# Output tiles of a gated MLP placed between the products of the next group, with PSUM banks of long and short use

## The chip, the cores and the metric

The kernel runs on one core of a Trainium2 chip. Its time is what the device takes for one execution, in microseconds (us). Five engines work side by side, each in its own program order: TensorE (PE, with its weight loads as PEld), VectorE (DVE), ScalarE (ACT), GpSimd (POOL) and SyncE (SP, which issues the transfers). An instruction starts when all before it on its engine have started and the semaphores that it names have been raised.

## What is computed

Clustered attention on 2 x 8 heads of 768 rows (1536 tokens of 512 values), then two MLPs without a bias; the change is in the second:

```python
def _moe_ref(x, w1, w2, w3, w_out):
    a = x @ w1
    b = x @ w2
    h = a * b @ w3
    return (h @ w_out).astype(np.float32)

def _moe2_ref(x, w_gate, w_val, w_out):        # 512 -> 1536 -> 512
    gate = 1.0 / (1.0 + np.exp(-(x @ w_gate)))
    val = x @ w_val
    return (gate * val @ w_out).astype(np.float32)
```

The weights of the MLPs come as 64-bit floats.

## The kernel before

Every matmul is done in three: each operand is split into a high part that the matmul takes exactly and a low part, and mm3 (L64 to L67) adds high x high, high x low and low x high into one PSUM bank. The high part is a copy or cast (by ACT or POOL), the low part a subtraction (by DVE or POOL).

**The second MLP** works on the 1536 hidden columns in six groups M of 256. For a group, `quads(M, 0)` makes the gates and `quads(M, 1)` the values. Each is a scheme of seven products (a to g) of half-size blocks in place of eight, once for each half p of the tokens: 14 products a0, a1, b0, b1, c0, c1, d0, e0, d1, e1, g0, f0, g1, f1, each 6 matmuls of 384 columns. Products a, c, e and g of one half add into one bank (names p4_..._a0, a1), b and f into another (b0, b1), d has its own (d0, d1). Partial sums are read between the steps: a **snapshot** s (ACT, L910) copies the a bank before the next product adds to it; DVE adds snapshots to later banks (L918, or L923) and, for the values, multiplies by the gate (L924, called a gate below). Of each finished block u = gate x value ACT then casts the high half (L929) and DVE subtracts the low half (L933). Twelve **output tiles** `out_unit(M, t)` of 128 tokens, 6 matmuls of 512 columns each, multiply u by the group's rows of w_out; DVE adds each to acc (L992; the first group's are copied by ACT, L990).

**The order around the change** is written out. The program of PE is a list of items (a product, or half a long one, or an output tile); `then(f, later)` puts f behind the item `later` places on, and `when(time, f)` puts f where the item at that time stands, on a clock of ticks, one tick being 12 matmuls of 512 columns. So the tables of times set the order on each engine, and the semaphores the rest. Before, the output tiles 0 to 5 of a group stand right behind its values, and 6 to 11 behind the gates of the next group:

```python
    for M in range(MG // GS):
        for w in range(2):
            ask_out(GS * M + w, at - 0.5)
            quads(M, w)
            if M or w:
                for t in range(6):
                    out_unit(M - 1 + w, t + 6 * (1 - w))
```

**Conversions.** A 64-bit weight tile is fetched by SP as raw words (512 KB), ACT takes two pieces of it (L836, L838), DVE clips, shifts and merges (L839, L842, L843, by way of a PSUM tile t), and POOL adds (L844). `ask_forms` then makes the seven weight forms: sums by POOL (L872), high halves by ACT (L886), low halves by POOL (L892). `ask_out` does the same for w_out.

**PSUM** has eight banks: six for products in one rotation (pool ps), two for t. A bank is used again when its last reader is done. **Before the second MLP**, the first one's last stage (`y_unit`) reads the split of g (`split_g`: high half by POOL or ACT, low half ghl by DVE, L59).

Of the kernel before, what the change touches and what calls it, by code (L numbers as in the profile page):

```python
# [27 lines left out]
def tile_cluster_attention__then__moe__then__gated_moe(  # L28
# [625 lines left out]

    def then(f, later=1):
        items[-1][1].append((later, f))
# [171 lines left out]
    def value_steps(src, name, key):  # L828
# [11 lines left out]
        yield  # L840
        t = cvp["pool"].tile([128, n], U32, tag="t", name=f"{name}_t", bufs=2)
        nc.vector.tensor_scalar(out=t, in0=a, scalar1=3, scalar2=0x3FFFFFF8, op0=ALU.logical_shift_left, op1=ALU.bitwise_and)  # L842
# [4 lines left out]
    def convert_at(time, src, name, key):  # L847
        steps = value_steps(src, name, key)
        for after in (-2.3, 0, 0.4, 1.0):
            when(time + after, lambda: next(steps, None))  # L850

    def ask_forms(M, w, start):
        key = (M, w)
        lead = 2.2 if M or w else 8.0
        for i in range(2):
            convert_at(start - lead - 2.8 + 1.2 * i, w_gv[2 * M + i, w], f"wgv{2 * M + i}_{w}", (key, i))
        half = [slice(0, 256), slice(256, 512)]
# [36 lines left out]

        for f, (pos, _, _) in A.items():
            time = start + pos * 6 * UNIT / TICK - lead
            if f in "bcef":
# [3 lines left out]

    def quads(M, w):
        key = (M, w)
# [9 lines left out]
        def combined(p, unit, mt, src, n):  # L913
# [12 lines left out]
            def hi():  # L926
                if (M, p, unit) not in us:
                    us[M, p, unit] = late["snap"].tile([128, GS, 2, UNIT], F32R, tag="u", name=f"u{M}_{p}_{unit}", bufs=4)
                nc.scalar.copy(us[M, p, unit][:, mt, 0], g)  # L929

            def lo():
                u = us[M, p, unit][:, mt]
                nc.vector.tensor_tensor(out=u[:, 1], in0=g, in1=u[:, 0], op=ALU.subtract)  # L933
# [6 lines left out]
            else:  # L940
                then(total)
                then(hi, 2)
                then(lo, 3)

        for step in "a0 a1 b0 b1 c0 c1 d0 e0 d1 e1 g0 f0 g1 f1".split():
            f, p = step[0], int(step[1])
            here = {"d": Y, "b": Z, "f": Z}.get(f, X)
            if f in "abd":
                here[p] = bank(f"p4_{M}_{w}_{f}{p}")[:, 0:UNIT]
            form = A[f][2]  # L950
            product(here[p], [lambda k=k, f=f: (a_hl[key, f][:, 0, 128 * k : 128 * k + 128], a_hl[key, f][:, 1, 128 * k : 128 * k + 128]) for k in range(2)],
                    [lambda k=k, p=p, form=form: y_form(p, form, k) for k in range(2)], f in "abd")
            if f == "a":
                then(snapshot(1, p))
            elif f == "c":
                then(snapshot(2, p))
# [10 lines left out]
    def ask_out(m, start):  # L967
        convert_at(start, w_out2[m], f"wo2_{m}", ("o", m))
# [5 lines left out]
        def lo():  # L974
            nc.gpsimd.tensor_tensor(out=wo2[m][:, 1], in0=outs["o", m], in1=wo2[m][:, 0], op=ALU.subtract)
        when(start + 2.0, hi)
        when(start + 2.3, lo)

    def out_unit(M, t):
        p, r = divmod(t, 6)  # L980
        unit, r = divmod(r, 3)
        tt = slice(128 * r, 128 * r + 128)
        bk = bank(f"p5_{M}_{t}")
        product(bk, [lambda i=i: (us[M, p, unit][:, i, 0, tt], us[M, p, unit][:, i, 1, tt]) for i in range(GS)],
                [lambda i=i: (wo2[GS * M + i][:, 0], wo2[GS * M + i][:, 1]) for i in range(GS)])
# [38 lines left out]
    for n, (work, posts, start, end) in enumerate(items):  # L1024
# [8 lines left out]
        work()  # L1033
        for f in due.pop(n, ()):
            f()
        while events and events[0][0] < end:
            events.pop(0)[2]()
        for later, f in posts:
            due.setdefault(n + later, []).append(f)
    for k in sorted(due):  # L1040
        for f in due[k]:
            f()
# [60 lines left out]
```

## Time and profile before

| | |
|---|---|
| median of 3 runs | 806.33 us (805.41 to 807.14) |
| the profiled execution, its own time | 806.35 us |
| its span, first to last instruction | 804.6 us |
| PE busy | 764.2 us (95%) |
| DVE, ACT, POOL busy | 558.5, 470.1, 399.6 us |
| mean granted clock of PE | 0.987 |

The views name an instruction by its line of the kernel, its engine and "output <- inputs" by tile names; a number in square brackets is the idle time of the engine before it and what ended it. A matmul's end is modelled, so that one is drawn longer than the distance to the next.

### The profile page before, as it was taken

How to read it: one execution, taken by the hardware profiler on the slowest of the kernel's cores; microseconds unless marked ns; L12 is line 12 of the kernel's file. 1: busy time of each engine (PE TensorE's matmuls, PEld its weight loads, DVE VectorE, ACT ScalarE, POOL GpSimd, SP SyncE). 2: the span in 40 equal slices, each digit the busy share in tenths (PEclk: the TensorE clock that was granted, in tenths of full speed). 3: DMA queues.
4: the chain of work that ended last, by engine and by line, in shares of the span. 5: the costliest groups of instructions: out<-in, count | busy, mean ns of one | idle time of the engine just before them, and what ended most of it. 6: DMA issues, size and time to landing. Idle time of an engine off the chain costs nothing.

```text
span 804.6 us, 12228 instructions
## 1 busy us (share of the span) xinstructions
PE 764.2 (95%) x4293; PEld 687.3 (85%) x4293; DVE 558.5 (69%) x895; ACT 470.1 (58%) x980; POOL 399.6 (50%) x418
## 2 busy tenths in 40 slices
PE   7999999998999999999999999989999899998997
PEld 7888888888998888888889988979889798897996
DVE  6798989898976665677642666574565856658555
ACT  3788788879885645455531354756654455454540
POOL 3447777777663456333320344835466354552540
PEclk9899999999999999999999999999999999999999
DMA  8766767666513333344320010312122120221004
GB/s 221 195 179 168 190 193 172 167 173 153 129 50 114 129 131 132 105 139 136 122 76 0 1 53 1 105 52 70 36 79 79 52 79 28 79 79 53 27 0 158
DMA packets 28893, 82.63 MB, mean 103 GB/s; under 512 B 4800, under 2 KB 4960, under 8 KB 28832
## 3 DMA queue, kind: packets, MB, share of 16 engines
q1 hardware_dynamic: 28832, 81.86, 34.4%
q8 instruction: 34, 0.56, 0.3%
q14 instruction: 27, 0.22, 0.1%
HBM read 52.49 MB, written 3.19 MB: 69 GB/s over the span
## 4 chain that ended last, share of the span: by engine, by line
PE 69%; DVE 14%; ACT 5%; issue 4%; DMA 3%; POOL 3%; SPq 1%; ACTq 0%; DVEq 0%; POOLq 0%
PE p L67 12%; PE p L66 11%; PE p L65 11%; PE pt L343 3%; PE p_a L65 3%; PE p_a L67 3%; PE p_a L66 3%; PE av L384 3%; DVE gate L924 2%; PE av L385 2%; DVE s L923 2%; PE w34p L65 2%; PE w34p L66 2%; PE w34p L67 2%; DMA xb<-xa 2%
## 5 line engine op out<-in xcount | busy, mean ns | idle before, releaser
L322 DVE TENSOR_REDUCE nm<-s 128x1 f32<-128x768 f32 x96 | 90.3, 942 | 11.4 <-PE s L315 10.9
L333 ACT ACTIVATE e<-s,nm 128x768 f32<-128x768 f32 x96 | 87.3, 909 | 14.6 <-DVE nm L322 13.9
L384 PE MATMUL av<-ph,vx 128*128 128x256 f32 x288 | 80.6, 309 | 11.1 <-ACT xa L393 10.5
L372 DVE TENSOR_TENSOR pl<-pt,ph 128x512 fp32r<-128x512 f32 x120 | 80.0, 682 | 11.6 <-ACT ph L361 10.3
L844 POOL TENSOR_TENSOR wgv_a<-wgv_f 128x512 uint32<-128x512 uint32 x24 | 26.6, 1108 | 120.2 <-ACT wgv_f L838 51.8
L361 ACT CAST ph<-pt 128x512 fp32r<-128x512 f32 x120 | 69.2, 593 | 23.5 <-PE pt L343 23.0
L343 PE MATMUL pt<-ident,e 128*128 128x128 f32 x576 | 80.2, 275 | 0.7 <-DVE pl L372 0.7
L67 PE MATMUL p<-x,w 128*128 128x512 f32 x192 | 74.7, 389 | 0.0
L66 PE MATMUL p<-x,w 128*128 128x512 f32 x192 | 74.7, 389 | 0.0
L65 PE MATMUL p<-x,w 128*128 128x512 f32 x192 | 74.7, 389 | 0.0
L343 PEld LDWEIGHTS pt<-ident,e 128*128 128x128 f32 x576 | 67.7, 143 | 5.8 <-PE pt L343 0.9
L385 PE MATMUL av<-pl,vx 128*128 128x256 f32 x288 | 72.6, 281 | 0.0
L67 PE MATMUL p<-wo,u 128*128 128x512 f32 x144 | 59.6, 414 | 13.1 <-DVE u L933 13.1
L384 PEld LDWEIGHTS av<-ph,vx 128*128 128x128 f32 x288 | 54.3, 188 | 18.9 <-ACT xa L393 8.8
L106 POOL TENSOR_TENSOR w_a<-w_f 128x512 uint32<-128x512 uint32 x32 | 34.7, 1085 | 62.6 <-DVE w_f L105 28.8
L66 PE MATMUL p<-wo,u 128*128 128x512 f32 x144 | 58.7, 407 | 0.0
L65 PE MATMUL p<-wo,u 128*128 128x512 f32 x144 | 58.7, 407 | 0.0
L385 PEld LDWEIGHTS av<-pl,vx 128*128 128x128 f32 x288 | 54.6, 190 | 0.1
L992 DVE TENSOR_TENSOR acc<-p,acc 128x512 f32<-128x512 f32 x60 | 40.6, 686 | 17.1 <-PE p L67 17.1
L929 ACT CAST u<-gate 128x384 fp32r<-128x384 f32 x48 | 24.6, 512 | 47.0 <-DVE gate L924 47.0
L910 ACT COPY s<-p_a 128x384 f32<-128x384 f32 x72 | 34.1, 475 | 27.9 <-PE p_a L67 27.8
L67 PEld LDWEIGHTS p<-wo,u 128*128 128x128 f32 x144 | 28.4, 197 | 21.8 <-DVE u L933 15.7
(229 smaller groups left out, 2315.5 us busy)
## 6 DMA issues: line engine op xcount, KB each, us to landing
wgv_f<-in_w_gv_dram SPq DMA_DIRECT2D x24, 512.0 KB, 3.2
wo_f<-in_w_out_dram SPq DMA_DIRECT2D x20, 512.0 KB, 3.2
w_f<-in_w_dram SPq DMA_DIRECT2D x16, 512.0 KB, 4.8
w_f<-in_w3T_dram SPq DMA_DIRECT2D x16, 512.0 KB, 4.2
raw<-in_qkT_dram SPq DMA_DIRECT2D x16, 384.0 KB, 3.2
vraw<-in_v_dram SPq DMA_DIRECT2D x8, 384.0 KB
QH<-hi SPq DMA_DIRECT2D x16, 192.0 KB, 4.7
KH<-hi SPq DMA_DIRECT2D x16, 192.0 KB, 3.6
```

What stands on the lines that cost most here:

```text
L65: nc.tensor.matmul(ps, whi, xhi, start=start, stop=False, skip_group_check=more)
L66: nc.tensor.matmul(ps, whi, xlo, start=False, stop=False, skip_group_check=more)
L67: nc.tensor.matmul(ps, wlo, xhi, start=False, stop=stop, skip_group_check=more)
L106: nc.gpsimd.tensor_tensor(out=a, in0=high, in1=low, op=ALU.add)
L322: nc.vector.tensor_reduce(out=nms[j], in_=sps[j][:, 0:S], axis=AX.X, op=ALU.max, negate=True)
L333: nc.scalar.activation(et, sps.pop(j)[:, 0:S], AF.Exp, bias=nms.pop(j), accum_out=acc_x[pr, "sum"][:, at : at + 1])
L343: nc.tensor.transpose(pt[:, kk, 128 * t : 128 * t + 128], exps[2 * i + t][:, k0 : k0 + 128], ident)
L361: nc.scalar.copy(ph, pt)
L372: nc.vector.tensor_tensor(out=pl, in0=src, in1=ph, op=ALU.subtract)
L384: nc.tensor.matmul(avs[i], w, ph[:, kk, :], start=kt == 0, stop=False)
L385: nc.tensor.matmul(avs[i], w, pl[:, kk, :], start=False, stop=kt == KT - 1)
L992: nc.vector.tensor_tensor(out=acc[:, t, :], in0=bk, in1=acc[:, t, :], op=ALU.add)
```

## The change

Output tiles no longer stand in rows of six. Group M's tiles 0 to 5 stand behind the sixth to eleventh product of the gates of group M+1, tiles 6 to 11 behind the products 1, 3, 4, 5, 6 and 7 (from 0) of its values; the last group keeps three of them for after its values, ahead of its own twelve. PSUM is divided anew: four long banks (a0, a1, b0, b1, each always the same one), three short ones (d and the output tiles), one for t. In the earlier stages the seven rotate. Posts behind an item get a second key (`turn`), by which snapshots come first; the cast of u's high half moves one item later, its low half one more. Conversions and forms get new times, w_out's are asked for within the values. split_g has 12 places for its halves in place of 10 (two of them in x's old memory), and splits four before the last unit in place of two.

```diff
-            t = cvp["pool"].tile([128, n], U32, tag="t", name=f"{name}_t", bufs=2)
+            t = cvp["pool"].tile([128, n], U32, tag="t", name=f"{name}_t", bufs=1)
...
-    def bank(name):
-        return ps.tile([128, 512], F32, tag="p", name=name)
+    LONG, SHORT = 4, 3
+    banks = 0
+
+    def bank(name, tag=None):
+        nonlocal banks
+        if not tag:
+            tag = "long" if banks % (LONG + SHORT) < LONG else "short"
+            banks += 1
+        return ps.tile([128, 512], F32, tag=tag, name=name, bufs=LONG if tag == "long" else SHORT)
...
-        hl = late["e"].tile([128, 2, UNIT], F32R, tag="e", name=f"ghl{v}_{m}", bufs=10)
+        n = (MF * v + m) % 12
+        if n < 10:
+            hl = late["e"].tile([128, 2, UNIT], F32R, tag="e", name=f"ghl{v}_{m}", bufs=10)
+        else:
+            hl = x_flat[:, PAIR * (n + 4) : PAIR * (n + 5)].rearrange("p (h c) -> p h c", h=2)
...
-                    when(at - 2 * half + 0.3 * k if k < 2 else at + half * (1 + (k > 5)), lambda k=k, v=v: split_g(v + 1, k))
+                    when(at - 2 * half + 0.4 * k if k < 4 else at + half, lambda k=k, v=v: split_g(v + 1, k))
...
-        lead = 2.2 if M or w else 8.0
+        if M == w == 0:
+            asked = (-10.8, -9.6)
+            ready = {f: A[f][0] * 6 * UNIT / TICK - 8.0 for f in A}
+        elif w == 0:
+            asked = (-6.2, -5.0)
+            ready = dict(a=-2.2, b=-1.6, c=-0.6, d=0.0, e=0.6, g=1.2, f=1.8)
+        else:
+            asked = (-5.0, -3.8) if M else (-4.6, -3.4)
+            ready = dict(a=-2.2, b=-1.8, c=-1.4, d=-1.0, e=-0.2, g=0.2, f=0.6)
...
-                then(hi, 2)
-                then(lo, 3)
+                then(hi, 3)
+                then(lo, 4, 2)
...
-                here[p] = bank(f"p4_{M}_{w}_{f}{p}")[:, 0:UNIT]
+                here[p] = bank(f"p4_{M}_{w}_{f}{p}", "short" if f == "d" else "long")[:, 0:UNIT]
...
-                then(snapshot(3, p))
+                then(snapshot(3, p), 1, 0)
...
+            for M_, t in (between or {}).get(n, ()):
+                out_unit(M_, t, "short")
...
+    LAST_M = MG // GS - 1
     for M in range(MG // GS):
-        for w in range(2):
-            ask_out(GS * M + w, at - 0.5)
-            quads(M, w)
-            if M or w:
-                for t in range(6):
-                    out_unit(M - 1 + w, t + 6 * (1 - w))
-    for t in range(6, 12):
-        out_unit(MG // GS - 1, t)
+        first = {5 + i: [(M - 1, i)] for i in range(6)} if M else {}
...
+        quads(M, 0, first)
...
+        then_tiles = {n: [(M - 1, 6 + i)] for i, n in enumerate((1, 3, 4, 5, 6, 7))} if M else {}
+        if M == LAST_M:
+            then_tiles = {n: [(M - 1, 6 + i)] for i, n in enumerate((1, 3, 4))}
+        quads(M, 1, then_tiles)
+    banks = 0
+    for t in range(9, 12):
+        out_unit(LAST_M - 1, t, "short")
+    for t in range(12):
+        out_unit(LAST_M, t)
```

**PE, end of the values of group 3.** Before, the last matmuls of product f1 (p4_3_1_b1) and then the group's first output tile (p5_3_0), which reads u:

```order
L65 MATMUL p4_3_1_b1_4095<-yb22_1_6081,a3_1_3_7628 128x384
L66 MATMUL p4_3_1_b1_4095<-yb22_1_6081,a3_1_3_7628 128x384
L67 MATMUL p4_3_1_b1_4095<-yb22_1_6081,a3_1_3_7628 128x384
L65 MATMUL p5_3_0_4098<-wo2_6_7404,u3_0_0_7655 128x512
L66 MATMUL p5_3_0_4098<-wo2_6_7404,u3_0_0_7655 128x512
L67 MATMUL p5_3_0_4098<-wo2_6_7404,u3_0_0_7655 128x512
```

In the changed kernel, the same place, where the first gate product of group 4 (p4_4_0_a0) follows:

```order
L65 MATMUL p4_3_1_b1_4090<-yb22_1_6085,a3_1_3_7536 128x384
L66 MATMUL p4_3_1_b1_4090<-yb22_1_6085,a3_1_3_7536 128x384
L67 MATMUL p4_3_1_b1_4090<-yb22_1_6085,a3_1_3_7536 128x384
L65 MATMUL p4_4_0_a0_4098<-x_153,a4_0_0_7676 128x384
L66 MATMUL p4_4_0_a0_4098<-x_153,a4_0_0_7676 128x384
```

The output tiles that stood there have moved six products on, and a0 needs a bank of the products just finished.

**DVE, the same tail.** Before, from the gate of g0 (it reads p4_3_1_a0) to the first low half of u that the output tile waits for (u3_0_0 from gate0_1); wgv8 and wgv9 are conversions:

```order
L924 TENSOR_TENSOR gate0_1_4016<-p4_3_1_a0_4092,gate0_1_4016 128x384
L842 TENSOR_SCALAR wgv8_0_t_7699<-wgv8_0_a_7661 128x512
L843 SCALAR_TENSOR_TENSOR wgv8_0_f64_7599<-wgv8_0_f64_7599,wgv8_0_t_7699 128x512
L933 TENSOR_TENSOR u3_1_1_7696<-gate1_1_4018,u3_1_1_7696 128x384
L923 TENSOR_TENSOR s3_1_2_0_7626<-p4_3_1_b0_4094,s3_1_2_0_7626 128x384
L924 TENSOR_TENSOR gate0_0_4015<-s3_1_2_0_7626,gate0_0_4015 128x384
L839 TENSOR_SCALAR wgv9_0_a_7703<-wgv9_0_a_7703 128x512
L933 TENSOR_TENSOR u3_0_0_7655<-gate0_1_4016,u3_0_0_7655 128x384
```

In the changed kernel, from the sum of d0 (L944 is the old L923, L945 the old L924, L952 the old L933, L1024 the old L992) to the gate of g1, which empties p4_3_1_a1:

```order
L1024 TENSOR_TENSOR acc_6078<-p5_2_11_4096,acc_6078 128x512
L952 TENSOR_TENSOR u3_0_0_7662<-gate0_0_4015,u3_0_0_7662 128x384
L944 TENSOR_TENSOR s3_1_1_1_7544<-p4_3_1_d1_4097,s3_1_1_1_7544 128x384
L945 TENSOR_TENSOR gate1_0_4017<-s3_1_1_1_7544,gate1_0_4017 128x384
L944 TENSOR_TENSOR s3_1_3_1_7696<-p4_3_1_b1_4090,s3_1_3_1_7696 128x384
L945 TENSOR_TENSOR gate1_1_4018<-s3_1_3_1_7696,gate1_1_4018 128x384
L952 TENSOR_TENSOR u3_0_1_7685<-gate0_1_4016,u3_0_1_7685 128x384
L945 TENSOR_TENSOR gate0_1_4016<-p4_3_1_a0_4086,gate0_1_4016 128x384
L944 TENSOR_TENSOR s3_1_2_0_7600<-p4_3_1_b0_4089,s3_1_2_0_7600 128x384
L945 TENSOR_TENSOR gate0_0_4015<-s3_1_2_0_7600,gate0_0_4015 128x384
L952 TENSOR_TENSOR u3_1_0_7710<-gate1_0_4017,u3_1_0_7710 128x384
L945 TENSOR_TENSOR gate1_1_4018<-p4_3_1_a1_4087,gate1_1_4018 128x384
```

No conversion stands between them any more, and one add of an output tile does.

**ACT, around the last snapshot of the values** (s3_1_3_1, of product e1). Before:

```order
L910 COPY s3_1_3_0_7657<-p4_3_1_a0_4092 128x384
L836 ACTIVATE wgv8_0_a_7661<-wgv8_0_f64_7599 128x512
L929 CAST u3_0_1_7670<-gate0_1_4016 128x384
L838 ACTIVATE wgv8_0_f64_7599<-wgv8_0_f64_7599 128x512
L929 CAST u3_1_0_7683<-gate1_0_4017 128x384
L910 COPY s3_1_3_1_7685<-p4_3_1_a1_4093 128x384
```

In the changed kernel (L931 is the old L910, L948 the old L929, L907 the old L886):

```order
L931 COPY s3_1_3_0_7660<-p4_3_1_a0_4086 128x384
L948 CAST u3_0_0_7662<-gate0_0_4015 128x384
L907 CAST a4_0_0_7676<-wgv8_0_a_7582 128x256
L948 CAST u3_0_1_7685<-gate0_1_4016 128x384
L907 CAST a4_0_0_7676<-sum4_0_b_7666 128x256
L931 COPY s3_1_3_1_7696<-p4_3_1_a1_4087 128x384
```

The cast of u3_1_0 no longer stands ahead of the snapshot; two casts of weight forms do, one of which reads a sum by POOL.

## Rows read from the trace of the kernel before

**Rows 1.** Busy times in a stretch: us, then PE, PEld, DVE, ACT, POOL, clock, DMA:

```profile
600.00:650.00 50.00, 46.83 (x237) 42.82 (x236) 33.59 (x58) 25.52 (x56) 25.22 (x32) 0.97 0.18 63
```

**Rows 2.** What PE waited for, whole span: us in total, times, longest:

```profile
PE p L67 <- DVE u L933: 13.1, 6, 2.5
...
PE p_a L65 <- ACT s L910: 4.0, 6, 0.7
PE p L66 <- DVE ghl L59: 2.7, 6, 1.4
```

**Rows 3.** Timeline of all engines at one wait for u: start, us, instruction:

```profile
627.98 0.47 ACT L910 COPY s<-p_a 128x384 f32<-128x384 f32 x1
...
630.70 0.39 PE L65 MATMUL p<-wo,u 128*128 128x512 f32 x1
...
631.20 0.69 DVE L843 SCALAR_TENSOR_TENSOR wgv_f<-wgv_f,wgv_t 128x512 uint32<-128x512 uint32 x1
...
631.63 0.40 PE L66 MATMUL p<-wo,u 128*128 128x512 f32 x1
...
632.02 1.23 POOL L844 TENSOR_TENSOR wgv_a<-wgv_f 128x512 uint32<-128x512 uint32 x1 [9.31 <-ACT wgv_f L838]
...
632.86 0.81 DVE L924 TENSOR_TENSOR gate<-s,gate 128x384 f32<-128x384 f32 x1
...
633.93 0.55 DVE L933 TENSOR_TENSOR u<-gate,u 128x384 fp32r<-128x384 f32 x1
...
634.53 0.71 PE L67 MATMUL p<-wo,u 128*128 128x512 f32 x1 [2.50 <-DVE u L933]
...
635.04 0.63 PE L65 MATMUL p<-wo,u 128*128 128x512 f32 x1
...
635.46 0.63 PE L66 MATMUL p<-wo,u 128*128 128x512 f32 x1
```

**Rows 4.** Busy times and clock (third number from the end) in chosen stretches:

```profile
400.00:500.00 100.00, 97.26 (x512) 89.98 (x511) 52.87 (x86) 36.25 (x78) 33.30 (x39) 1.00 0.08 28
...
534.20:539.10 4.90, 4.84 (x14) 3.87 (x15) 4.83 (x9) 2.35 (x6) 1.27 (x2) 0.65 0.25 94
...
736.30:740.50 4.20, 4.16 (x11) 3.30 (x12) 4.13 (x8) 1.33 (x3) 0.66 (x1) 0.59 0.29 110
```

**Rows 5.** Timeline: output tiles, then products, undisturbed:

```profile
612.22 0.39 PE L67 MATMUL p<-wo,u 128*128 128x512 f32 x1
...
614.94 0.39 PE L67 MATMUL p<-wo,u 128*128 128x512 f32 x1
...
617.27 0.33 PE L65 MATMUL p_b<-x,a 128*128 128x384 f32 x1
...
621.98 0.73 POOL L892 TENSOR_TENSOR a<-sum_f,a 128x256 fp32r<-128x256 f32 x1
...
622.30 0.33 PE L67 MATMUL p_d<-x,a 128*128 128x384 f32 x1
...
622.74 0.56 DVE L923 TENSOR_TENSOR s<-p_d,s 128x384 f32<-128x384 f32 x1 [5.17 <-PE p_d L67]
```

**Rows 6.** Groups by line and shape, 500 us to the end: busy us, mean ns:

```profile
L992 DVE TENSOR_TENSOR acc<-p,acc 128x512 f32<-128x512 f32 x60 | 40.6, 686 | 17.1 <-PE p L67 17.1
...
L924 DVE TENSOR_TENSOR gate<-s,gate 128x384 f32<-128x384 f32 x36 | 21.3, 592 | 1.2
```

**Rows 7.** Timelines of DVE and POOL: low halves of g beside POOL, and without:

```profile
447.14 1.02 DVE L59 TENSOR_TENSOR ghl<-g,ghl 128x384 fp32r<-128x384 f32 x2
...
481.50 3.64 DVE L59 TENSOR_TENSOR ghl<-g,ghl 128x384 fp32r<-128x384 f32 x4 [2.75 <-POOL ghl L54]
...
481.91 1.04 POOL L892 TENSOR_TENSOR a<-sum_c,a 128x256 fp32r<-128x256 f32 x1
```

**Rows 8.** Who waited for whom, 500 us to the end: us in total, times, longest:

```profile
ACT a L886 <- POOL sum_b L872: 22.2, 9, 2.9
```

**Rows 9.** Transfers by line: KB each, us from issue to landing:

```profile
wgv_f<-in_w_gv_dram SPq DMA_DIRECT2D x24, 512.0 KB, 3.2
```

More of the change, by code (lines that the diff above doesn't have):

```diff
@@ L653, in item, with then @@
         at += columns / TICK
-    def then(f, later=1):
-        items[-1][1].append((later, f))
+    def then(f, later=1, turn=1):
+        items[-1][1].append((later, turn, f))
     def when(time, f):
         events.append((time, len(events), f))
-    def bank(name):
-        return ps.tile([128, 512], F32, tag="p", name=name)
+    LONG, SHORT = 4, 3
[6 more added lines that the diff above has]
+        return ps.tile([128, 512], F32, tag=tag, name=name, bufs=LONG if tag == "long" else SHORT)
     def product(p, w, x, first=True, halves=1):
@@ L848, in convert_at @@
         steps = value_steps(src, name, key)
-        for after in (-2.3, 0, 0.4, 1.0):
+        for after in (-2.0, 0, 0.4, 1.0):
             when(time + after, lambda: next(steps, None))
@@ L853, in ask_forms @@
         key = (M, w)
-        lead = 2.2 if M or w else 8.0
+        if M == w == 0:
[7 more added lines that the diff above has]
+            ready = dict(a=-2.2, b=-1.8, c=-1.4, d=-1.0, e=-0.2, g=0.2, f=0.6)
+            if M == 0:
+                ready.update(b=-1.5, c=-1.1, d=-0.7)
         for i in range(2):
-            convert_at(start - lead - 2.8 + 1.2 * i, w_gv[2 * M + i, w], f"wgv{2 * M + i}_{w}", (key, i))
+            convert_at(start + asked[i], w_gv[2 * M + i, w], f"wgv{2 * M + i}_{w}", (key, i))
         half = [slice(0, 256), slice(256, 512)]
@@ L893, in lo @@
             return work
-        for f, (pos, _, _) in A.items():
-            time = start + pos * 6 * UNIT / TICK - lead
+        for f in A:
+            time = start + ready[f]
             if f in "bcef":
@@ L900, in ask_forms, with quads @@
             when(time + 0.3, lo(f))
-    def quads(M, w):
+    def quads(M, w, between=None):
         key = (M, w)
@@ L926, in hi @@
             def hi():
-                if (M, p, unit) not in us:
-                    us[M, p, unit] = late["snap"].tile([128, GS, 2, UNIT], F32R, tag="u", name=f"u{M}_{p}_{unit}", bufs=4)
-                nc.scalar.copy(us[M, p, unit][:, mt, 0], g)
+                nc.scalar.copy(u_of(M, p, unit, mt)[:, 0], g)
             def lo():
-                u = us[M, p, unit][:, mt]
+                u = u_of(M, p, unit, mt)
                 nc.vector.tensor_tensor(out=u[:, 1], in0=g, in1=u[:, 0], op=ALU.subtract)
@@ L941, in combined @@
                 then(total)
-                then(hi, 2)
-                then(lo, 3)
-        for step in "a0 a1 b0 b1 c0 c1 d0 e0 d1 e1 g0 f0 g1 f1".split():
+                then(hi, 3)
+                then(lo, 4, 2)
+        for n, step in enumerate("a0 a1 b0 b1 c0 c1 d0 e0 d1 e1 g0 f0 g1 f1".split()):
             f, p = step[0], int(step[1])
@@ L953, in quads @@
             if f == "a":
-                then(snapshot(1, p))
+                then(snapshot(1, p), 1, 0)
             elif f == "c":
-                then(snapshot(2, p))
+                then(snapshot(2, p), 1, 0)
             elif f == "d":
@@ L965, in quads, with u_of, ask_out @@
                 combined(p, 1, 0, Z[p], 2)
-    def ask_out(m, start):
+            for M_, t in (between or {}).get(n, ()):
+                out_unit(M_, t, "short")
+    def u_of(M, p, unit, mt):
+        key = (M, p, unit)
+        if key not in us:
+            if key == (MG // GS - 1, 1, 1):
+                us[key] = [words["pool"].tile([128, 512, 2], F32R, tag="f64", name=f"u{M}_{p}_{unit}_{i}", bufs=3) for i in range(GS)]
+                us[key] = [t.rearrange("p n t -> p (n t)")[:, 0 : 2 * UNIT].rearrange("p (h c) -> p h c", h=2) for t in us[key]]
+            else:
+                t = late["snap"].tile([128, GS, 2, UNIT], F32R, tag="u", name=f"u{M}_{p}_{unit}", bufs=4)
+                us[key] = [t[:, i] for i in range(GS)]
+        return us[key][mt]
+    def ask_out(m, start, split_at):
         convert_at(start, w_out2[m], f"wo2_{m}", ("o", m))
@@ L975, in lo, with out_unit @@
             nc.gpsimd.tensor_tensor(out=wo2[m][:, 1], in0=outs["o", m], in1=wo2[m][:, 0], op=ALU.subtract)
-        when(start + 2.0, hi)
-        when(start + 2.3, lo)
-    def out_unit(M, t):
+        when(split_at, hi)
+        when(split_at + 0.3, lo)
+    def out_unit(M, t, tag=None):
         p, r = divmod(t, 6)
@@ L982, in out_unit @@
         tt = slice(128 * r, 128 * r + 128)
-        bk = bank(f"p5_{M}_{t}")
-        product(bk, [lambda i=i: (us[M, p, unit][:, i, 0, tt], us[M, p, unit][:, i, 1, tt]) for i in range(GS)],
+        bk = bank(f"p5_{M}_{t}", tag)
+        product(bk, [lambda i=i: (us[M, p, unit][i][:, 0, tt], us[M, p, unit][i][:, 1, tt]) for i in range(GS)],
                 [lambda i=i: (wo2[GS * M + i][:, 0], wo2[GS * M + i][:, 1]) for i in range(GS)])
@@ L1033, in tile_cluster_attention__then__moe__then__gated_moe @@
         work()
-        for f in due.pop(n, ()):
+        for _, f in sorted(due.pop(n, ()), key=lambda x: x[0]):
             f()
@@ L1037, in tile_cluster_attention__then__moe__then__gated_moe @@
             events.pop(0)[2]()
-        for later, f in posts:
-            due.setdefault(n + later, []).append(f)
+        for later, turn, f in posts:
+            due.setdefault(n + later, []).append((turn, f))
     for k in sorted(due):
-        for f in due[k]:
+        for _, f in sorted(due[k], key=lambda x: x[0]):
             f()
```

10 lines of the change are left out of this document (8 added, 2 removed).

## The prediction

> **What bounds the kernel now.** I read the busy times by stage first. In the second MLP TensorE (PE) is busy 46.8 of every 50 us while the next busiest engine, VectorE (DVE), has 33.6 [rows 1]. So PE sets the time, and only three things can shorten the run: time in which PE waits, time at the lower clock, and fewer matmuls. The matmul count does not change. Then the list of PE's waits: three of its lines lie in the stages that the change touches [rows 2]. Then the timeline around the longest of them [rows 3]: the value products of a group end, the first output tile starts at once with the high half of u, and its third matmul needs u's low half. DVE is still working off that group's gates and, between them, a weight conversion (L843 at 631.20). PE issued at 631.63 and next at 634.53. After that its matmuls are 0.42 us apart (635.04 to 635.46), against 0.23 elsewhere [rows 5]. The windows say why [rows 4]: over such a stretch the granted clock has a mean of 0.59 or 0.65, a mix of its two levels, 2.4 and 1.2 GHz, behind a stop of 2.5 us.
>
> **What there is to win.**
> - The wait for u: 13.1 us in six places, five of 2.5 and one of 0.6 [rows 2]. The list counts from a matmul's modelled end, but matmuls overlap: at 512 columns one issues every 2.72/12 = 0.227 us and is drawn 0.39 long [rows 5]. So each stop costs 0.16 more: 13.1 + 6 x 0.16 = 14.1.
> - The wait for the snapshot s (ScalarE, ACT, L910): 4.0 + 6 x 0.16 = 5.0 us [rows 2].
> - The half clock: 4.9 us x (1 - 0.65) = 1.7 us [rows 4] and 4.2 x (1 - 0.59) = 1.7 for the last; four such stretches in all, behind four of the five long stops, each of the same loss: 6.8 us.
> - The wait for ghl in the stage before: 2.7 + 6 x 0.16 = 3.7 us [rows 2].
>
> Sum 29.6 us. As a check from below: a product of 384 columns is 6 matmuls 0.173 us apart (5.03 us over 29 intervals), 1.04 us; an output tile 6 x 0.227 = 1.36 us [rows 5]. One group is 28 x 1.04 + 12 x 1.36 = 45.4 us, six groups 272.6.
>
> **The change part by part.**
>
> *Output tiles between products.* A tile of group M now stands in group M+1, at the earliest six products (6.2 us) behind the last value product. In the trace u's low half was done 633.93 + 0.55 = 634.5, some 3.8 us after the first output matmul (630.70 by the order; the first one shown is 631.63) and with conversions in the queue. So u is ready with some 2 us to spare, and the 14.1 us go, with the 6.8 us behind them. The last group has three tiles of the group before as cover, 4.1 us; it has no conversions and waited for 0.6 us only. PE's work is the same.
>
> *Snapshots before casts.* hi is cast one step later and the snapshot goes first among posts of a step. In the order of ACT the snapshot of e1 stood behind a cast that waits for DVE's gate; now it stands behind casts whose gates are two steps older. 5.0 us go.
>
> *Four early halves of g (split_g).* Two more buffers, four early splits in place of two, so that the second half-product has 4.1 us for four low halves, which cost 0.51 us each with GpSimd (POOL) idle and 0.91 with it busy [rows 7]: 2.0 to 3.6 us. I take 0.4 of the 3.7 us as staying, with 0 to 3.7 as ends.
>
> *One conversion bank in place of two.* t is written and read by neighbouring DVE instructions, which run one after the other anyway. Cost 0; it would be 0.69 us a conversion only if another engine used t. In the stages ahead banks rotate over seven in place of six, and PE waits for none there [rows 2]; the last group's u takes two buffers that no conversion needs any more. Both 0.
>
> *Conversions earlier.* Their raw words are asked for 2.0 ticks (a tick is 12 matmuls of 512 columns, 2.72 us) ahead, 5.4 us, against 3.2 us to land [rows 9]. The SP queue passes no other transfer of this stage but the output's, at the end. They leave the tail of the value products on DVE, where the merge alone cost 0.69 each [rows 3], and go into its quieter middle. ACT stands still in front of sum_b, 22.2 us in nine places, at most 2.9 [rows 8]; the sigmoid that frees a gate bank stands behind such a cast and has 3.0 us to spare. By the same count along POOL's order the weights for the next a0 are ready some 1.8 us early, which pays for four of POOL's at 0.3 more each. Cost 0 by both ends.
>
> *Four long, three short banks: the new wait.* Before, six output tiles (8.2 us) stood between the last value product and the next a0. Now a0 follows f1 at once, in the bank that DVE must have emptied. Count from the a0 of the values: the outputs at six places give d0 end 12.72, e0 15.12, d1 17.52, e1 18.56, g0 19.60, f0 20.64, g1 21.68, f1 22.72, and the next a1 starts at 23.76. DVE sees a product 0.27 us after PE issues the next (622.74 against 622.30 + 0.17) [rows 5]. Along DVE's order, with 0.59 where an instruction needs the one before it and 0.69 for an output [rows 6], and 0.47 where it doesn't (two low halves took 1.02, the second 0.55 of it) [rows 7]: gate d0 done 14.8, snapshot of e0 ready 15.87, u's first low half 18.0, gate of d1 19.0, snapshot of e1 ready 18.56 + 0.27 + 0.47 = 19.30, so its sum at 19.35; then gate, low half, gate of g0 (a0's bank, done 21.4, wanted 22.6), sum and gate of f0, a low half, gate of g1 done 23.45. a1's load wants it at 23.6. The slack is 0.15 us: next to none, in five places (behind groups 0 to 4).
>
> What eats it is POOL. Its sums and low halves for the next weights used to start behind the tail; POOL idled 9.31 us until 632.02 [rows 3]. Now they lie beside it. A DVE instruction with two SBUF inputs took 0.81 beside POOL's at 632.86 against 0.55 alone [rows 3]; with POOL packed, four took 3.64, 0.91 each, against 1.02 for two alone, and POOL's own took 1.04 for 0.73 [rows 7]. Of DVE's instructions ahead of g1's gate, eight have two SBUF inputs, of which some five lie beside POOL. At +0.26: 1.3 us, less the slack 0.15 and the 0.4 that the wait for e1's snapshot absorbs: 0.75. At +0.40: 1.5. At nothing: 0. I take 0.75 + 0.16 = 0.9 in five places, 4.5 us, nearer to the lower price because POOL pauses when ACT's casts make it wait. Behind group 0, where no output tiles stretch the tail, it may be up to 1.9. Ends: 0 and 8.5 us. A stop of 1.4 us for ghl left the clock of 400:500 at 1.00 [rows 2, 4], so no half clock is added.
>
> The Trainium skill (SBUF — State Buffer, "Who interferes with whom") says that a DVE instruction with two SBUF inputs contends with a GpSimd instruction that reads SBUF, and its rules for authors that the second to issue fully blocks until the first has finished. By that rule the place is right, but the price is the rest of a whole POOL instruction, and the sum would be that of the second rival below; the 0.81 and 0.91 here are shorter than 0.55 + 0.73.
>
> Sum: 29.6 - 0.4 - 4.5 = 24.7 us. The profiled execution took 806.35 us by its own time (span 804.6), the median of the runs 806.33, so they are the same. 806.35 - 24.7 = 781.7 (rounded up).
>
> **The rivals.**
> - *No new wait at all.* For it: a slack above zero by the count. Against it: POOL's rows. 806.35 - 29.6 = 776.8.
> - *Slower: DVE blocked.* Place: the gate of g1, before the next a1. If each of the eight instructions waits for a whole POOL instruction of 0.73, the gate comes 8 x 0.73 - 0.55 = 5.3 us late, and with 0.16 five times 27.3 us; four of five stops bring the half clock, 6.8 us: 776.8 + 34.1 = 810.9. It decides from 5.9 us a place on, clock included (29.6 / 5). Against it: 0.81 and 0.91, not 1.28. In between, five instructions blocked in full, 3.1 us a place, give 776.8 + 16.3 + up to 6.8 = 793 to 800.
> - *The stall only moves.* The conversions in the middle of the values delay d0's bank, and with three short banks an output tile must wait for the add of the third one before. For it: three banks where there were six. Against it: between a short bank's end and its next use lie at least 3.4 us of products, for an add of 0.69. If it waits 2.5 us twelve times: 776.8 + 30 = 807, no change.
>
> **How the numbers follow.** Forecast with its ends (0.5 to 9 us of waits left, 777.5 to 786): 0.62. No new wait, 776 to 777.5: 0.15. Partly blocked, 786 to 800: 0.15. Unchanged, within 0.2% (1.6 us, about what a measurement of this kernel can tell): 0.03. Slower: 0.05. To leave out no more than 2 in 10 the range goes from 775.5 to 791: below the cap by 1.3 us, for the rounding in 18 stops at 0.16 and in the four half-clock stretches.
>
> **What would show it.** Right: no PE wait for u; p_a's wait for s gone; clock 1.00 throughout the last 300 us; a group every 46 to 47 us; five new waits of p_a for DVE's gate, 0.3 to 1.6 us each, at the second product of groups 1 to 5. Wrong: such waits of 2.5 us and more with half-clock stretches behind them; a wait of an output tile for DVE's add; a wait of the products for a (the converted weights).

## The result and the profile after

The changed kernel takes 780.24 us in the median of 4 runs (779.41 to 781.97), the kernel before 806.55 beside it (4 runs); the ratio is 0.9678 [0.9658, 0.9699]. The forecast was 781.7. The profiled execution took 780.68 us (span 778.9), 25.7 less than the 806.35 of before. Line numbers of the changed kernel are those of the order rows above (L931 snapshot, L944 and L945 sum and gate, L948 and L952 the halves of u, L1024 the add of an output tile).

PE's waits, whole span (the answer to [rows 2]):

```profile
PE p_a L65 <- ACT s L931: 2.0, 1, 2.0
PE p L66 <- DVE ghl L59: 0.7, 3, 0.2
```

The line for u is gone, and no wait for the gate has come. The six waits for a snapshot, one in the values of each group, are gone too; the one shown is new, in the gates of group 0, and longer than any of the six. Windows (columns as in [rows 1]), which answer to [rows 1, 4]:

```profile
475.00:525.00 50.00, 47.31 (x258) 45.80 (x257) 31.65 (x50) 29.89 (x66) 33.95 (x41) 0.97 0.22 74
525.00:775.00 250.00, 250.00 (x1299) 231.00 (x1297) 189.86 (x302) 136.58 (x294) 130.66 (x146) 1.00 0.18 64
600.00:650.00 50.00, 50.00 (x264) 46.53 (x263) 40.03 (x63) 30.09 (x65) 30.01 (x35) 1.00 0.19 67
```

From 525 us to its last matmul PE is never drawn idle and the clock stays at 1.00; 264 matmuls fit where 237 did. What is left lies in the first window. Where the gain came from is read off PE's timeline by stage: the first matmul of the stage that reads ghl, the first of the second MLP, the last of all. Before:

```profile
428.90 0.33 PE L65 MATMUL p<-ghl,w 128*128 128x384 f32 x1
...
500.18 0.33 PE L65 MATMUL p_a<-x,a 128*128 128x384 f32 x1
...
800.45 0.39 PE L67 MATMUL p<-wo,u 128*128 128x512 f32 x1
```

After, with the a0 of group 5's gates besides:

```profile
428.10 0.33 PE L65 MATMUL p<-ghl,w 128*128 128x384 f32 x1
...
496.37 0.33 PE L65 MATMUL p_a<-x,a 128*128 128x384 f32 x1
...
712.91 0.33 PE L65 MATMUL p_a<-x,a 128*128 128x384 f32 x1
...
774.78 0.39 PE L67 MATMUL p<-wo,u 128*128 128x512 f32 x1
```

The second MLP shrank from 300.3 to 278.4 us (21.9), the ghl stage from 71.3 to 68.3 (3.0), and 0.8 lie ahead of both.

**The new stop.** Timelines of the first group's gates, one engine after the other:

```profile
503.48 0.34 PE L67 MATMUL p_d<-x,a 128*128 128x384 f32 x1
505.85 0.44 PE L65 MATMUL p_a<-x,a 128*128 128x384 f32 x1 [2.04 <-ACT s L931]
506.13 0.34 PE L66 MATMUL p_a<-x,a 128*128 128x384 f32 x1
...
503.53 0.62 ACT L1004 CAST wo<-wo_a 128x512 fp32r<-128x512 f32 x1 [1.55 <-POOL wo_a L855]
504.76 0.67 ACT L847 ACTIVATE wgv_a<-wgv_f 128x512 f32<-128x512 f32 x1 [0.61 <-POOL wo L1007]
505.33 0.85 ACT L931 COPY s<-p_a 128x384 f32<-128x384 f32 x2
...
502.46 1.04 POOL L855 TENSOR_TENSOR wo_a<-wo_f 128x512 uint32<-128x512 uint32 x1
503.46 2.50 POOL L1007 TENSOR_TENSOR wo<-wo_a,wo 128x512 fp32r<-128x512 f32 x2
...
500.00:520.00 20.00, 17.96 (x94) 17.64 (x94) 11.93 (x20) 15.34 (x34) 16.21 (x19) 0.91 0.28 93
```

The last line is the window around the stop, with a mean granted clock of 0.91, a mix of the two levels of 2.4 and 1.2 GHz. PE may not add e0 to the a0 bank before the snapshot is taken. ACT stands still 1.55 us in front of a cast of w_out, because POOL has not merged that weight, and 0.61 us more in front of the next conversion. The snapshot is behind both. So a conversion that was placed anew, not a product, holds PE. The stop costs 505.85 - 503.48 - 0.17 = 2.20, the matmul behind it 0.11 more (506.13 - 505.85 = 0.28 for 0.17), and one stretch at the lower clock some 1.7 by [rows 4] (the window gives 20 x 0.09 = 1.8).

**Where a wait was forecast.** The end of group 3's values, DVE, POOL and PE:

```profile
665.63 0.55 DVE L945 TENSOR_TENSOR gate<-p_a,gate 128x384 f32<-128x384 f32 x1
666.10 0.55 DVE L944 TENSOR_TENSOR s<-p_b,s 128x384 f32<-128x384 f32 x1
...
667.25 1.09 DVE L952 TENSOR_TENSOR u<-gate,u 128x384 fp32r<-128x384 f32 x1
668.27 0.54 DVE L945 TENSOR_TENSOR gate<-p_a,gate 128x384 f32<-128x384 f32 x1
...
670.82 1.09 DVE L952 TENSOR_TENSOR u<-gate,u 128x384 fp32r<-128x384 f32 x1
...
666.88 1.06 POOL L893 TENSOR_TENSOR sum_e<-wgv_a 128x256 f32<-128x256 f32 x1
...
667.07 0.33 PE L65 MATMUL p_a<-x,a 128*128 128x384 f32 x1
668.11 0.33 PE L65 MATMUL p_a<-yb,a 128*128 128x384 f32 x1
669.15 0.33 PE L65 MATMUL p_b<-x,a 128*128 128x384 f32 x1
...
674.46 0.40 PE L67 MATMUL p<-wo,u 128*128 128x512 f32 x1
```

a1 started at 668.11, and the gate of g1 that reads the old a1 bank ended at 668.27 + 0.54 = 668.81. So a1 was not in that bank. It took the one that b0 had left (its last reader, the sum at 666.10, was done at 666.65), and the late bank went to b0, which starts at 669.15, 0.34 us after the gate. The four long banks are one pool, handed out in the order in which they come free; in `e4_old_casts` below b0 indeed waits for this gate. The description of the change above said that each product always has the same one: that is wrong. The last low half of u that the group's first tile needs, that of g0, was done at 670.82 + 1.09 = 671.91. Its reader is the tile's sixth matmul, the one that waited in the kernel before (634.53 in [rows 3]); it starts at 674.46, so 2.55 us are to spare.

### The profile page after: what moved, and what is told of

Read it like the earlier page. It is cut to its first block, busy times and chain, and to the rows that moved or that the text cites. A ratio compares the mean times of both kernels' runs of the same rounds, so it can differ in the third digit from the quotient of the medians.

```text
span 778.9 us, 12205 instructions
## 1 busy us (share of the span) xinstructions
PE 754.6 (97%) x4293; PEld 683.5 (88%) x4293; DVE 575.4 (74%) x895; ACT 470.6 (60%) x980; POOL 410.8 (53%) x418
## 4 chain that ended last, share of the span: by engine, by line
PE 78%; DVE 6%; ACT 4%; issue 4%; DMA 3%; POOL 3%; SPq 2%; ACTq 0%; DVEq 0%; POOLq 0%
PE p L67 12%; PE p L66 12%; PE p L65 12%; PE p_a L65 4%; PE p_a L66 4%; PE p_a L67 4%; PE pt L343 4%; PE av L384 3%; PE av L385 2%; SPq L62 2%; PE p_b L65 2%; PE p_b L66 2%; PE p_b L67 2%; PE w34p L67 2%; PE w34p L65 2%
## 5 line engine op out<-in xcount | busy, mean ns | idle before, releaser
L65 PE MATMUL p<-x,w 128*128 128x512 f32 (+1 forms) x208 | 80.0, 385 | 0.0
L67 PE MATMUL p<-x,w 128*128 128x512 f32 (+1 forms) x208 | 80.0, 385 | 0.0
L66 PE MATMUL p<-x,w 128*128 128x512 f32 (+1 forms) x208 | 80.0, 385 | 0.0
L1024 DVE TENSOR_TENSOR acc<-p,acc 128x512 f32<-128x512 f32 x60 | 41.2, 687 | 29.9 <-PE p L67 29.5
L931 ACT COPY s<-p_a 128x384 f32<-128x384 f32 x72 | 34.4, 479 | 44.3 <-PE p_a L67 43.9
L67 PE MATMUL p<-wo,u 128*128 128x512 f32 x144 | 57.0, 396 | 0.0
L66 PE MATMUL p<-wo,u 128*128 128x512 f32 x144 | 56.7, 394 | 0.0
L65 PE MATMUL p<-wo,u 128*128 128x512 f32 x144 | 56.0, 389 | 0.0
L66 PEld LDWEIGHTS p<-x,w 128*128 128x128 f32 x208 | 39.1, 188 | 7.5
L67 PEld LDWEIGHTS p<-x,w 128*128 128x128 f32 x208 | 39.1, 188 | 7.5
```

The costliest lines, as they stand in the source:

```text
L65: nc.tensor.matmul(ps, whi, xhi, start=start, stop=False, skip_group_check=more)
L66: nc.tensor.matmul(ps, whi, xlo, start=False, stop=False, skip_group_check=more)
L67: nc.tensor.matmul(ps, wlo, xhi, start=False, stop=stop, skip_group_check=more)
L1024: nc.vector.tensor_tensor(out=acc[:, t, :], in0=bk, in1=acc[:, t, :], op=ALU.add)
```

## Experiments

All but `e9_casts_alone` are the changed kernel with edits. Times are medians, the ratio is to the kernel before on the same chip.

**Own banks.** Every product gets its own bank, as the prediction had assumed (in the earlier stages, too, the four long banks are now four fixed ones; that part of the edit is not shown).

```diff
-                here[p] = bank(f"p4_{M}_{w}_{f}{p}", "short" if f == "d" else "long")[:, 0:UNIT]
+                here[p] = bank(f"p4_{M}_{w}_{f}{p}", "short" if f == "d" else f"long{2 * (f == 'b') + p}")[:, 0:UNIT]
```

> a0, a1, b0 and b1 get a PSUM bank each for good; the rest is the changed kernel. Theory (the pool hands the bank that came free first to the next product, so a1 gets b0's old bank and the gate of g1 has one product more time): now a1 of groups 1 to 5 waits for that gate, drawn 0.8 to 0.9 us, 1.0 with the overlap, in five places: 785.2. The prediction's rows would say the same of the wait itself (0.75 + 0.16 each, 784.7). Rival (DVE is in time anyway): no such wait, 780.2.

784.24 us, 0.9727 [0.9711, 0.9744]; 785.2 was expected. The list of waits, and one of the five (PE):

```profile
PE p_a L65 <- DVE gate L946: 3.0, 5, 0.9
...
670.82 0.45 PE L65 MATMUL p_a<-yb,a 128*128 128x384 f32 x1 [0.60 <-DVE gate L946]
```

The forecast waits are there, in the forecast places, 0.28 to 0.89 us each (forecast 0.75 drawn). What spared the changed kernel is the order in which banks are handed out. The 4.0 us between the medians are not the price of these five alone: in group 0 the stop of 2.04 us and its lower clock are gone here (clock 1.00 from 495 to 520 us), with stops of 1.05, 0.73 and 0.26 us in their place. The next kernel has the same three, so the five are priced against that one.

**No low halves beside the tail.** The kernel above, without POOL's low halves of the gates' weight forms in groups 1 to 5; the product reads the high half in their place (this edit is not shown), so that part of the sum is left out.

```diff
+                if M and not w:
+                    return
                 t = a_hl[key, f]
                 nc.gpsimd.tensor_tensor(out=t[:, 1], in0=source(f), in1=t[:, 0], op=ALU.subtract)
```

> The kernel in which a0, a1, b0 and b1 have a bank each, without POOL's low halves of the gates' weight forms of groups 1 to 5; the products read the high half in their place, so the output is another. Theory (POOL beside DVE's gates makes those with two SBUF inputs late): the gate of g1 is 0.5 to 0.8 us earlier, and the waits of a1 for it fall from 3.0 us in five places (0.3 to 0.9) to 0.5 us or less in all: 780.5 to 781.5 against 784.2. Rival (DVE is late by its own queue): the waits stay at 2.5 to 3 us and the time at 784.

780.32 us, 0.9674 [0.9659, 0.9688]; all five waits for the gate are gone from the list. POOL's sums are done earlier too (at group 3's end by 663.4 us, with the gate of g1 at 667.3), so nothing of POOL lies beside the tail. So the waits were the price of POOL beside DVE. The two second MLPs differ by 4.2 us (281.7 and 277.5, by first and last matmul as above) for 3.0 us drawn: a stop costs some 0.24 more than it is drawn, where the prediction added 0.16. The 0.11 of the next matmul is the rest.

**The split of w_out later.** Only the times at which the two tiles of w_out are cast in group 0's gates.

```diff
-                ask_out(w, at - 1.2 + w, at + 0.6 + 0.6 * w)
+                ask_out(w, at - 1.2 + w, at + 0.2 + 2.8 * w)
```

> Only the splits of the first two w_out tiles move: the first 0.4 ticks earlier, the second 1.8 ticks later, behind the snapshots of the first gates. Theory (ACT stood in front of a cast that waited for POOL, and the snapshot of c0 behind it): the one wait of 2.0 us of p_a for s at 505.85 us goes, and the half-clock stretch behind it; 2.0 + 0.16 + 1.7 = 3.9 us less than the changed kernel's 780.2, so 776.3. Rival (the snapshot is late for another reason, the gate or the buffer of the conversion): the wait stays above 1 us and the time within 779 to 781.

779.47 us, 0.9668 [0.9648, 0.9687], where 776.3 was expected. The long stop is gone and the window 500 to 520 is at clock 1.00; three small ones came (PE):

```profile
513.33 0.44 PE L65 MATMUL p_b<-x,a 128*128 128x384 f32 x1 [0.24 <-DVE gate L939]
...
515.92 0.44 PE L65 MATMUL p_a<-x,a 128*128 128x384 f32 x1 [0.21 <-ACT s L931]
...
517.58 0.44 PE L65 MATMUL p_a<-yt,a 128*128 128x384 f32 x1 [0.34 <-ACT s L931]
```

Two more kernels try for those. In the first the second split stands between the two places:

```diff
-                ask_out(w, at - 1.2 + w, at + 0.6 + 0.6 * w)
+                ask_out(w, at - 1.2 + w, at + 0.2 + 1.7 * w)
```

> The changed kernel with the second split of w_out in group 0 at 1.9 ticks, between the place in the changed kernel (1.2) and that of e1_split_later (3.0). Theory: ACT's casts wait for POOL only where the cast is asked for before POOL's merge of the same weight; from 1.9 on it does not, and POOL's low half no longer lies between the forms of the values, so neither the 2.0 us stop with its half clock nor the three small ones of 0.8 us are there: 780.68 - 3.9 = 776.8 in the profile, 778 in the median. Rival: the stop returns in part, because the raw words' merge on POOL is late there: 779 to 780.

778.78 us, 0.9649 [0.9636, 0.9662], the fastest of all kernels here by its median (778 was expected without any stop). One stop of 0.47 us is left in the second MLP:

```profile
510.95 0.44 PE L65 MATMUL p_a<-x,a 128*128 128x384 f32 x1 [0.47 <-ACT s L931]
```

In the other, DVE makes the second low half of w_out in place of POOL (`nc.vector` for `nc.gpsimd` where m is 1), with the late place kept:

> e1_split_later with the second low half of w_out of group 0 done by DVE in place of POOL. If POOL's 1.3 us for it is what made the three small waits of e1 (0.8 us drawn, 1.3 with the distance), they go: 778.36 - 1.3 = 777 in the profile and 778.2 in the median. If they come from DVE's or ACT's order, they stay, or grow by up to 0.7 us where DVE is late with a gate: 779.5 to 780.2.

779.26 us, 0.9658 [0.9645, 0.9671], where 778.2 was expected; of three stops one of 0.33 is left, so POOL's low half made two of them and not the third. By first and last matmul the second MLP takes 278.4 us in the changed kernel, 276.3 with the late place, 275.3 and 275.4 in these two. With 0.7 for the stop that is left in the kernel between, the long stop and its clock cost 3.1 + 0.7 = 3.8 us (3.9 by the rows). Between medians only 0.8 to 1.5 show, and the intervals touch that of the changed kernel: stages ahead of the change vary by one or two us between executions.

**Casts and snapshots as before**, all else changed.

```diff
-                then(hi, 3)
-                then(lo, 4, 2)
+                then(hi, 2)
+                then(lo, 3)
...
-                then(snapshot(3, p), 1, 0)
+                then(snapshot(3, p))
```

> Casts and low halves of u one step earlier again and snapshots in the old order among posts; the rest is the changed kernel. Theory (a cast that waits for DVE's gate held up the snapshot of e1): PE's wait of p_a for s returns in five or six places at 0.7 us, 0.86 with the overlap: 784.5 to 785.4. Rival (with the conversions out of the tail the gates come early enough): 780.2 to 781.

796.64 us, 0.9873 [0.9852, 0.9893]: a miss by 11 us. PE's waits, and DVE and PE at one of them:

```profile
PE p_a L65 <- ACT s L931: 7.2, 8, 1.9
PE p_b L65 <- DVE gate L945: 5.9, 5, 1.2
...
531.01 0.55 DVE L945 TENSOR_TENSOR gate<-p_a,gate 128x384 f32<-128x384 f32 x1
531.47 0.55 DVE L952 TENSOR_TENSOR u<-gate,u 128x384 fp32r<-128x384 f32 x1
...
533.56 1.08 DVE L952 TENSOR_TENSOR u<-gate,u 128x384 fp32r<-128x384 f32 x1
534.57 0.55 DVE L945 TENSOR_TENSOR gate<-p_a,gate 128x384 f32<-128x384 f32 x1
...
535.17 0.44 PE L65 MATMUL p_b<-x,a 128*128 128x384 f32 x1 [1.20 <-DVE gate L945]
```

Two low halves (531.47 and 533.56) now stand between the gate of g0 and that of g1, where the changed kernel has one, so the gate of g1 ends 4.1 us after the other starts, against 3.2 at the end of group 3 above (665.63 to 668.81); at the end of group 3 it is 4.1 here, too. The gate of g0 is itself some 0.8 us later against PE: at the end of group 3 it is done 0.13 us before a0 starts, in the changed kernel 0.89 (666.18 and 667.07). The two make 1.7 us, the slack was 0.34, and b0 waits at every group. Snapshots stand behind casts again, 0.6 us each. The 11.1 us drawn more than in the changed kernel, with 0.24 for each of 12 more stops, make 14 of the 15.8 that the second MLP grew; the rest is not assigned. So the late gate, and not the snapshots alone, is what the expectation had missed.

**The gates' conversions as late as before**, with their forms at the old times.

```diff
-            asked = (-6.2, -5.0)
-            ready = dict(a=-2.2, b=-1.6, c=-0.6, d=0.0, e=0.6, g=1.2, f=1.8)
+            asked = (-5.0, -3.8)
+            ready = {f: A[f][0] * 6 * UNIT / TICK - 2.2 for f in A}
```

> The changed kernel, with the gates' conversions of groups 1 to 5 asked for 1.2 ticks later, at the old distance, and their forms at the old times. Theory (the early times keep conversions out of DVE's tail): a clip, a shift and a merge, 0.42 + 0.68 + 0.69, come back between the gates, so that the gate of g1 is 1.2 to 1.8 us later and b0 of groups 2 to 5, which takes its bank, waits 0.9 to 1.5 us, 1.1 to 1.7 with the overlap: 784.6 to 787. Rival (the tail has slack enough): 780 to 781.5.

785.87 us, 0.9747 [0.9732, 0.9761]. PE's new wait, and the window 500 to 520:

```profile
PE p_a L65 <- DVE gate L945: 2.2, 3, 0.8
...
500.00:520.00 20.00, 17.97 (x104) 17.65 (x103) 12.55 (x22) 16.69 (x37) 16.70 (x19) 1.00 0.33 105
```

Conversions in DVE's tail delay the gates that free banks. The waits are not where they were expected: a0 of groups 3 to 5 waits 0.74 to 0.76 us for the gate of g0, and not b0 of groups 2 to 5 for that of g1; four waits of b products, 0.8 us in all, come besides. The new times are worth 5.6 us between the medians. In the profiled executions the second MLP is 3.9 longer, though the stop of 2.03 us that it shares with the changed kernel brought no lower clock here.

**Rows of six again**, first with the old casts, then with the new ones (all other parts changed).

```diff
-        quads(M, 0, first)
+        quads(M, 0)
+        for t in range(6, 12):
+            if M:
+                out_unit(M - 1, t, "short")
...
-        quads(M, 1, then_tiles)
+        quads(M, 1)
+        for t in range(6):
+            out_unit(M, t, "short")
```

> Output tiles stand in rows of six again, right behind the values and the gates, with the old casts of u; the new times of the conversions, banks and split_g stay. Theory (the place of the tiles carries most, the conversions in DVE's tail made the stop long): PE waits for u again in six places, but for 0.7 to 1.5 us in place of 2.5, and for s as in the run with the old casts: 790 to 796. Rival (the conversions alone made the wait): no wait for u, 780 to 786. Rival (the place is all): 2.5 us and the half clock again, 800 to 806.

818.21 us, 1.0141 [1.0109, 1.0172]. PE's waits:

```profile
PE p_a L65 <- ACT s L931: 14.8, 7, 2.5
PE p L67 <- DVE u L952: 11.0, 6, 2.8
```

> Output tiles in rows of six as in the run before, but with u's casts one step later, its low halves last in their step, and snapshots first. So it is the changed kernel but for the place of the tiles (and low halves one step earlier, since the tile behind reads them). Theory (the late casts free ACT for the snapshots, the place of the tiles frees PE of the wait for u): p_a's wait for s falls from 14.8 us in seven places to 2 in one; the wait for u stays at 2 to 2.8 us in five: 798 to 806. Rival (casts alone carry it): under 790. Rival (the place alone): 815 to 818 again.

825.29 us, 1.0237 [1.022, 1.0254]. PE's waits, and DVE ahead of one of those for u:

```profile
PE p L67 <- DVE u L952: 20.6, 6, 4.1
PE p_b L65 <- DVE s L944: 8.4, 5, 1.9
...
584.59 0.69 DVE L853 TENSOR_SCALAR wgv_t<-wgv_a 128x512 uint32<-128x512 uint32 x1
...
589.08 0.54 DVE L952 TENSOR_TENSOR u<-gate,u 128x384 fp32r<-128x384 f32 x1
```

Both are misses: 790 to 806 was expected, and both are slower than the kernel before. The conversion times count from the next gates. With six tiles standing ahead of those, the same numbers put a conversion into the tail of the values again, as in the kernel before. In the second kernel the tile behind them waits up to 4.1 us, where it waited 2.5 [rows 2]. Part of the rise is the later cast, since the new casts alone make it 3.3 (next run); another part is POOL's work that now lies beside the tail, where the gate at 586.50 takes 1.18 us and the low half at 587.61 1.08, for 0.55 alone. How much each has was not tested. So these two do not price the place of the tiles by itself, and no other run does: with the tiles put back, the wait for u is back, but place and times only work together.

**Casts alone.** The kernel before with the snapshots first and the casts of u one step later (hi 3, lo 3 behind the rest).

> The kernel before with one part of the change: snapshots first among posts, u's casts one step later and its low halves last in their step. Theory (the snapshot of e1 stood behind a cast that waits for DVE's gate): p_a's wait for s goes, 4.0 us in six places, 5.0 with the overlap; the wait for u stays near 13 us or grows by up to 0.5 a place, since the cast of u comes later: 801 to 805. Rival (what is won on the snapshot is lost on u): 805 to 807, no difference.

804.15 us, 0.9972 [0.9962, 0.9982]: the time is in the expected 801 to 805, the wait for u is not. The wait for s is gone, and that for u has grown from 13.1, by 0.84 us in each of the five long places, where up to 0.5 was expected:

```profile
PE p L67 <- DVE u L933: 17.5, 6, 3.3
```

So most of what the snapshots win is lost again on u; the second MLP is 1.3 us shorter (299.0 after 300.3).

**split_g as before**, ten places and two early halves.

```diff
-                    when(at - 2 * half + 0.4 * k if k < 4 else at + half, lambda k=k, v=v: split_g(v + 1, k))
+                    when(at - 2 * half + 0.3 * k if k < 2 else at + half * (1 + (k > 5)), lambda k=k, v=v: split_g(v + 1, k))
```

> The changed kernel with split_g as before (ten places, two early halves in place of four). If the four early halves are what took the wait of the output units for ghl from 2.7 us in six places to 0.7 in three, it comes back: 2.0 us plus 3 x 0.16, so 780.2 + 2.5 = 782.7, with no half clock and the second MLP unchanged at 278.4 us. If the wait went because banks rotate over seven in place of six there, it stays at 0.7 and the time at 780.2.

783.39 us, 0.9712 [0.9699, 0.9725]. Its wait, the window behind its longest stop, and the window of the stop of 2.03 that it shares with the changed kernel:

```profile
PE p L66 <- DVE ghl L59: 2.7, 6, 1.4
...
465.00:475.00 10.00, 8.14 (x36) 7.50 (x35) 5.85 (x9) 3.96 (x9) 4.12 (x4) 0.83 0.06 13
...
500.00:520.00 20.00, 17.97 (x104) 17.65 (x103) 13.66 (x25) 15.19 (x33) 14.06 (x16) 1.00 0.31 105
```

The wait is the 2.7 us of before, so the change of split_g (places and early halves together) is what took it, and not the seventh bank. The time is 0.7 above the expected 782.7, but its parts differ: the long stop in front of ghl brought a lower clock, which was not expected, and the second MLP took 276.8 us, not 278.4.

**Two short banks** in place of three (`LONG, SHORT = 4, 2`).

> The changed kernel with two short PSUM banks in place of three (six rotate in the earlier stages). With two, three tiles of a group must take the bank that the short product one item before has just left: one product of 1.04 us lies between, for DVE's sight of the end (0.27) and an add of 0.69, or 0.96, and more if DVE has something else in front. Theory (three banks have slack, two don't): waits of 0.2 to 1.0 us in 15 places, 3 to 15 us, 784 to 795, with 788 the likeliest. Rival (the stall only moves, banks were the limit already): 807 and more. If short banks play no part at all: 780.2.

786.37 us, 0.9744 [0.9725, 0.9762]. The new wait, and one of its places (PE):

```profile
PE p L65 <- DVE acc L1024: 3.5, 5, 0.9
...
591.67 0.50 PE L65 MATMUL p<-wo,u 128*128 128x512 f32 x1 [0.65 <-DVE acc L1024]
```

It waits in five places of the 15 thought possible: the tile behind d1 in the gates of groups 2 to 5, and once behind the last values. With two banks the add is 0.65 to 0.87 us too late there, with three it never is.

## Why the prediction was right, and where it was not

- *What there is to win, 29.6 us.* The wait for u (14.1) went whole, the four half-clock stretches behind it too (6.8), with u 2.55 us early where "some 2 us to spare" was forecast (the prediction's "third matmul" is the tile's sixth). The group takes 712.91 - 667.07 = 45.84 us, by the check from below 45.4; the sign named 46 to 47.
- *Snapshots before casts, 5.0.* All six waits went, so the size holds. Without the new order of casts, the second MLP is 15.8 us longer: beside interleaved tiles the low halves stand ahead of the gate that frees a bank. The prediction saw the snapshots and not this.
- *split_g: 0.4 left.* 0.7 us in three places are left, 1.2 with their distance, and the stage won 3.0, 0.5 more than the 2.5 that the waits account for. That the change of split_g did it is shown by undoing it.
- *Conversions earlier: "cost 0 by both ends".* This step failed. It was argued from the conversions of the gates behind groups 0 to 4; that of w_out in group 0 got a new time as well, and there ACT waits for POOL with a snapshot behind it. It costs 2.2 + 1.7 = 3.9 us in the profiled execution, and moving the cast alone takes the stop away.
- *Four long banks: the new wait, 4.5 us.* This step failed too, by its premise that a0, a1, b0 and b1 each wait for their own bank. The count of DVE's tail was good: the gate of g1 was to end 24.2 us after the a0 of the values with POOL's share, and a1 was to start at 23.76; in group 3, counted from 644.15, they came at 24.66 and 23.96. With own banks the wait is 0.6 in three of five places. But the banks go round, and the forecast wait is 0.

Sum of the terms, with the old waits counted as gone in full: 14.1 + 5.0 + 6.8 + 3.7 won, less the new stop with its clock (3.9) and 1.2 at ghl, makes 24.5; the stages show 21.9 + 3.0 = 24.9, and 0.8 came from elsewhere. So the 29.6 us to win were rightly seen, but that the 24.7 of the forecast came so close was luck: a wait of 4.5 that did not come stood in for one of 3.9 that was not seen.

- *The rivals.* "No new wait at all" is what happened at the group's end, though not in time. "The stall only moves" is refuted: three short banks have slack, and two cost 6 us, not 27. "DVE blocked" needs a correction. The prediction set the rule aside because 0.81 and 0.91 are shorter than 0.55 + 0.73. That test was wrong, since the second instruction waits only for the rest of the first. In the rows above the low half of u starts at 667.25, while POOL's sum runs from 666.88 to 667.94, and ends at 668.34, 0.40 later. In the second MLP of the changed kernel's timeline 43 DVE instructions with two SBUF inputs (gates from s, and low halves of u) start more than 0.01 us after one of POOL's and over 0.2 us before its end, and all end 0.41 to 0.42 us after it, however long that was. Five more start within 0.01 us of POOL's, take their 0.55 us, and POOL's takes 1.14 to 1.15 for 0.74. The 0.81 of [rows 3] fits, too (632.86 + 0.81 = 633.67; POOL 632.02 + 1.23 = 633.25). So the Trainium skill (SBUF — State Buffer, "Who interferes with whom") has it right that the second is held until the first is done, and the trace agrees with it. What failed in the rival was its price: the rest of POOL's instruction, 0.24 to 0.77 in these 43, and not a whole one eight times over.

## What to carry to other kernels

An engine's stop is filled by work that needs nothing from the stage before; but with the cover used up, the orders around it weigh more: that of the casts was worth 2.4 us in the kernel before and 16 in this one, and the times of the conversions 5.6 here. So the parts of such a change have to be priced together. A bank pool that hands out what comes free first forgave one late bank here, and banks fixed by name did not. When many times in a table move, follow the moved ones that happen once, as in the first group, as closely as those that repeat.

## What was not expected of the hardware

- *The clock after equal stops.* The stop at e0 of group 0 was 2.03 to 2.05 us in five kernels. In the changed kernel and with two short banks a stretch of lower clock followed (0.85 in the window 500 to 510 of the first); with old conversion times and old split_g none did (1.00 in the windows shown), nor with rows of six and new casts (1.00 from 500 to 520), and with old split_g the second MLP is 1.6 us shorter than the changed kernel's. With the old casts a stop of 1.88 us did bring one (0.91 from 500 to 520). In the stage before, a stop of 1.4 left the clock at 1.00 in the kernel before [rows 4], and 0.83 stands in the window of the same stop above. So the half clock behind one stop is a price that may or may not fall due.
- *DVE and POOL hold each other up in turn.* A sum or low half by POOL that starts within such a DVE instruction, with over 0.3 us of it to run, ends 0.60 to 0.61 us after it (25 cases in the changed kernel's second MLP, 0.94 to 1.13 long for 0.74), and a DVE one behind it that starts within POOL's waits for that. DVE's sums and gates that read PSUM kept their 0.54 to 0.56 beside POOL (24 cases), as the gate at 668.27 did.
